# A fused RWKV, MoE and SoLU kernel: a unit's y moves one MLP step forward, next to its state update

## The chip, the cores and the metric

The kernel runs on one core of a Trainium2 chip. The metric is device time in microseconds (us) of one execution, the median of several runs.

## The reference, cut to what matters

```python
for t in range(S):                                  # S = 768, batch 4, 8 heads of 48
    cur = einsum('bhd,bhe->bhde', u[None] * kt, vt)
    y[:, :, t] = einsum('bhd,bhde->bhe', rt, state + cur)
    state = wt[:, :, :, None] * state + einsum('bhd,bhe->bhde', kt, vt)
x = y.transpose(0, 2, 1, 3).reshape(3072, 384)
h = x @ w_in                                        # 384 -> 2048
x = (h - tanh(h)) @ w_out                           # 2048 -> 384
h = x @ w_in2                                       # 384 -> 1024
solu = h * softmax(h)
out = layernorm(solu, eps=1e-6) * g_ln @ w_out2     # 1024 -> 384
```

## The kernel before, in words

The recurrence is cut into 24 units of 128 time steps (`C`), six to a batch row. A unit is five pieces of work. `att_0` brings w and r into the transposed form, makes the running product of w (`inc`) and scales r with it (`rh`). `att_1` makes the scaled k (`kh`). `att_2` puts the diagonal into `aq` on GpSimd, multiplies kh with rh on TensorE (`qk`), writes the masked products into `aq` on VectorE (line 303), transposes kh (`kt`), and copies that to `kn` on ScalarE. `att_3` multiplies kn with v (`ds`) and adds that to the old state, which gives the next state `st`; the last unit of a batch row has no such work. `att_4` makes y out of rh times the old state (line 340) and aq times v (line 343). It then copies y as a rounded high part and a rest into `xs` and `x3` (ScalarE lines 345 and 346, VectorE lines 347 and 348), and moves x3 into the 16-row remainders of xs with six DMAs (line 351). The old state that att_4 reads is the one from which att_3 starts; the two write and read different state buffers.

The first MLP works on blocks of 512 tokens, four units each, in 16 steps of 128 hidden columns: 96 steps in all, numbered s. In step s, `part1` multiplies xs of the block with the weights `wa` (`hp`, 9 matmuls of 512 columns). ScalarE, VectorE and GpSimd then make g out of hp (lines 386 to 398; VectorE's two instructions are lines 387 and 392). `part2` multiplies the g of step s-2 with the second weights (`x2p`, 9 matmuls), and adds up in three PSUM banks. There are two hp buffers and three g buffers. In the first and the last block the polynomial goes through hp itself, so hp is held until line 392 has read it; in the others line 387 is its last reader.

The attention of the first four units is done ahead of the MLP. That of units 4 to 23 is spread over the MLP's steps by the loop below, four steps to a unit, and always works for the block behind the one that is being multiplied. `xs` has two buffers, one for even blocks and one for odd ones. A block's first hp can start only when the DMAs of its last unit (units 7, 11, 15, 19, 23) have landed in xs. In the first 14 steps the loop also loads and converts the first MLP's weights (`conv_a`: DMA into `raw`, ScalarE line 121, VectorE lines 129 to 131, ScalarE line 134, GpSimd line 135 into `wa`). `raw` has two buffers. In the last block the second MLP's weights are converted in the same way (`conv_b`). The second MLP stage follows (lines 466 and 544), and is not touched.

The written order is not what the engines get: a scheduler reorders the instructions of each engine by a modelled time, with the written order as priority. All DMAs are issued by SyncE's queue (SP), which issues them in that scheduled order and holds each until what it waits for is done.

Of the kernel before, what the change touches and what calls it, by code (L numbers as in the profile page):

```python
# [559 lines left out]
@with_exitstack  # L560
def rwkv_moe_moe_kernel(ctx: ExitStack, tc: tile.TileContext, *args):
    nc = tc.nc
    K = Kern(tc, args)
    const = ctx.enter_context(tc.tile_pool(name="const", bufs=1))
    dram = ctx.enter_context(tc.tile_pool(name="dram", bufs=1, space=bass.MemoryType.DRAM))
    K.x2d = dram.tile([DM, NT], F32, name="x2d")
    safe = fast_path(tc, K, const)
    ok = nc.values_load(safe, min_val=0, max_val=1)
    with tc.If(ok < 1):
        general_path(tc, K, const)  # L570


def fast_path(tc, K, const):
    nc = tc.nc

    def pool(stack, name, bufs=1, side=None, **kw):
        return stack.enter_context(tc.tile_pool(name=name, bufs=bufs, side=side, reuse_waits="tile", **kw))

    K.load_act_set()
    K.setup(const)  # L580
    K.gl = const.tile([128, NM2], F32, name="gl")
    L, R, R2 = ExitStack(), ExitStack(), ExitStack()
    cv = pool(L, "cv", 2)
    cvr = pool(L, "cvr", 2)
    K.gp = pool(L, "gp", 2)
    K.gs = pool(L, "gs", 3)
    wp = pool(L, "wp")
    xp1 = pool(L, "xp1")
    xp0 = pool(R, "xp0", side="right")
    att = pool(R, "att", side="right")  # L590
    ps_x = pool(L, "ps_x", space=PSUM)
    K.ps_h = pool(L, "ps_h", 2, space=PSUM)
    K.ps_a = pool(R, "ps_a", 3, side="right", space=PSUM)
    K.wa = wp.tile([128, 2, NM, 2 * DM], F32R, name="wa")
    K.x2p = [ps_x.tile([128, BLK], F32, name=f"x2p{d}") for d in range(KM)]
    K.att_setup(att, xp0, xp1)
    K.setup_mask(K.kh[0])

    raw, gs = {}, {}
    OFF = -18  # L600
    LAST = (NB - 1) * NM
    nc.sync.dma_start(out=K.ub, in_=K.u.rearrange("h d -> (h d)").partition_broadcast(128))
    nc.scalar.activation(K.ub, K.ub, AF.Copy, scale=-1.0)
    K.att_load(0)
    K.att_load(1)
    nc.sync.dma_start(out=K.gl, in_=K.g_ln.rearrange("(k p) -> p k", p=128))

    early = 2
    when = (0, 2, 3, 5, 6, 8, 9, 11)
    SK = 2.1  # L610
    first = [(k + SK * u, K.att_pre if k < 0 else getattr(K, f"att_{k}"), u) for u in range(UB) for k in range(-1, 5)]
    first += [(SK * (u - 2) + 1.05, K.att_load, u) for u in range(2, UB + 2)] + [(SK * UB - 1, K.att_pre, UB)]
    first += [(2.0 * m, lambda m: K.conv_a(cv, cvr, m), m) for m in range(early)]
    for _, f, n in sorted(first, key=lambda e: e[0]):
        f(n)
    for s in range(-2, NB * NM + 2):
        if 0 <= s < NB * NM:
            gs[s] = K.part1(*divmod(s, NM))
        for k in (4, 0, 1, 2, 3):
            u, rem = divmod(s - OFF - k, 4)  # L620
            if rem == 0 and UB <= u < NU:
                getattr(K, f"att_{k}")(u)
        u, rem = divmod(s - OFF + 1, 4)
        if rem == 0 and UB < u < NU:
            K.att_pre(u)
        u, rem = divmod(s - OFF + 6, 4)
        if rem == 0 and UB + 1 < u < TURN:
            K.att_load(u)
        u, rem = divmod(s - OFF + 3, 4)
        if rem == 0 and TURN <= u < NU:  # L630
            K.load_turned(u)
        if 0 <= s - 2 < NB * NM:
            K.part2(*divmod(s - 2, NM), gs.pop(s - 2))
        if 0 <= s < NM - early:
            K.conv_a(cv, cvr, s + early)
        if s == LAST:
            R.close()
            wb = pool(R2, "wb", side="right")
            K.bx = pool(R2, "bx", 2, side="right")
            K.wb = wb.tile([128, 2, NM2, 2 * DM], F32R, name="wb")  # L640
            ps_r = pool(R2, "ps_r", side="right", space=PSUM)
        if s - LAST in when:
            with tc.issue_after(K.last_dve.ins), tc.issue_after(K.last_act.ins):
                K.conv_b(cv, cvr, when.index(s - LAST))
        if s == LAST + NM - 2:
            big = [
                cvr.tile([128, 2, DM, 2], U32, tag="raw", name=x).rearrange("p i f two -> p (i f two)")
                .bitcast(F32)[:, 0:FF2].rearrange("p (f x) -> p f x", f=2)
                for x in ("e0", "so0")
            ]  # L650
            K.ps_b, K.exps = (ps_r,), []
            small = K.ub.rearrange("p h d -> p (h d)")
            hs = {0: K.b_h(K.load_x2(0), 0, None, (small[:, 0:8], small[:, 8:40], *big))}
        n, due = divmod(3 * (s - NM), 7)
        if 0 <= n < NM + NM2 and due < 3:
            K.check_pair(cvr, n)
    safe = K.safe_flag(const)
    L.close()

    K.bs = pool(L, "bs", 5)  # L660
    K.bp = pool(L, "bp", 3)
    K.dso = pool(L, "dso", 3, space=bass.MemoryType.DRAM)
    ps_l = pool(L, "ps_l", space=PSUM)
    ps_t = pool(L, "ps_t", space=PSUM)
    K.ps_b = (ps_r, ps_t, ps_l)
    ts = {}
    for n in range(NTT + 3):
        if n < NTT:
            if n > 0:
                hs[n] = K.b_h(K.load_x2(n), n, (lambda: ts.update({n - 2: K.b_w(ts[n - 2])})) if n >= 2 else None)  # L670
            if K.shuffled(n):
                ts[n] = K.b_s(hs[n][0])
        if 0 <= n - 1 < NTT and not K.shuffled(n - 1):
            ts[n - 1] = K.b_t(hs[n - 1][0])
        if 0 <= n - 3 < NTT:
            K.b_o(n - 3, ts.pop(n - 3), hs.pop(n - 3)[1])
    L.close()
    R2.close()
    return safe
# [196 lines left out]
```

## Time and profile before

| | us |
|---|---|
| median of 3 runs | 796.96 (796.57 to 797.53) |
| the profiled execution, its own time | 795.77 |
| span of the profiled execution | 794.0 |
| TensorE busy with matmuls | 738.7 |
| VectorE, ScalarE, GpSimd busy | 592.7, 498.3, 418.7 |
| mean granted TensorE clock, share of full | 0.985 |

The span is what the trace shows; the profiled execution's own time is 1.77 us more. TensorE is the busiest engine by far, and is idle for the remaining 55.3 us of the span.

### The profile page before, as it was taken

What the parts mean: (1) busy time and instruction counts of PE and PEld (TensorE: products, weight loads), DVE (VectorE), ACT (ScalarE), POOL (GpSimd) and SP (SyncE); (2) the same over time, 40 slices, a digit from 0 to 9 for tenths busy, and PEclk for the clock granted to TensorE, in tenths of its full rate; (3) what the DMA queues carried; (4) which work ended last, traced back from release to release, by engine and by line L of the source; (5) the groups of instructions that cost most, each with busy time, mean ns of one, the idle gap of its engine ahead of it and who ended that gap; (6) DMA issues with size and microseconds to landing.
All of it is one profiled execution on the core that took longest, in us unless ns stands there. A gap on an engine that the chain in (4) does not pass through costs nothing. (4 is left out here: it accounts for less than half of the span.)

```text
span 794.0 us, 13215 instructions
## 1 busy us (share of the span) xinstructions
PE 738.7 (93%) x4338; PEld 604.9 (76%) x4338; DVE 592.7 (75%) x1023; ACT 498.3 (63%) x944; POOL 418.7 (53%) x389
## 2 busy tenths in 40 slices
PE   3677989889999999999999999999999999999997
PEld 2565767668887777778787777776878899898886
DVE  4689978777786677767676676368559999989982
ACT  3435776587776776687767765588736455554552
POOL 3544656556665555557555565366715544555440
PEclk9978998999999999999999999999999999999999
DMA  9965663867567575776646530043034554655531
GB/s 162 180 100 126 130 178 87 194 164 192 138 154 174 167 173 138 174 185 164 173 126 192 145 95 26 29 137 108 13 123 167 178 183 154 191 177 168 182 104 45
DMA packets 178158, 113.12 MB, mean 142 GB/s; under 512 B 95520, under 2 KB 166816, under 8 KB 178080
## 3 DMA queue, kind: packets, MB, share of 16 engines
q1 hardware_dynamic: 178080, 112.19, 54.1%
q8 instruction: 36, 0.59, 0.3%
q14 instruction: 42, 0.34, 0.2%
HBM read 88.81 MB, written 20.97 MB: 138 GB/s over the span
## 5 line engine op out<-in xcount | busy, mean ns | idle before, releaser
L381 PE MATMUL hp<-xs,wa 128*128 128x512 f32 x864 | 222.0, 400 | 9.6 <-DVE y L392 3.9
L405 PE MATMUL x2p<-g,wa 128*128 128x512 f32 x864 | 224.0, 399 | 6.7 <-ACT g L395 4.4
L381 PEld LDWEIGHTS hp<-xs,wa 128*128 128x128 f32 x864 | 162.5, 191 | 49.4 <-POOL wa L135 7.9
L405 PEld LDWEIGHTS x2p<-g,wa 128*128 128x128 f32 x864 | 158.2, 188 | 46.1 <-ACT g L395 6.0
L398 POOL TENSOR_TENSOR g<-y,g 128x512 fp32r<-128x512 f32 x96 | 128.5, 1339 | 39.3 <-ACT g L395 30.4
L387 DVE TENSOR_TENSOR y<-hp,t 128x512 f32<-128x512 f32 x96 | 65.6, 685 | 87.5 <-ACT t L386 86.2
L466 PE MATMUL h<-wb,x2s 128*128 128x512 f32 x432 | 106.1, 399 | 2.4 <-POOL x2s L451 2.4
L544 PE MATMUL o<-wb,ts 128*128 128x384 f32 x576 | 104.7, 335 | 1.0 <-POOL ts L523 1.0
L393 ACT ACTIVATE q<-t,cst 128x512 f32<-128x512 f32 x96 | 69.4, 723 | 53.7 <-DVE y L392 53.2
L544 PEld LDWEIGHTS o<-wb,ts 128*128 128x128 f32 x576 | 100.4, 188 | 3.3 <-POOL ts L523 1.3
L466 PEld LDWEIGHTS h<-wb,x2s 128*128 128x128 f32 x432 | 80.7, 188 | 21.8 <-POOL x2s L451 3.3
L397 POOL TENSOR_SCALAR g<-y 128x512 fp32r<-128x512 f32 x64 | 39.6, 619 | 94.7 <-DVE y L392 90.9
L386 ACT ACTIVATE t<-hp 128x512 f32<-128x512 f32 x96 | 56.5, 590 | 36.2 <-PE hp L381 35.7
L523 POOL TENSOR_TENSOR ts<-tw,ts 128x512 fp32r<-128x512 f32 x44 | 58.1, 1342 | 7.2 <-ACT ts L522 7.1
L392 DVE SCALAR_TENSOR_TENSOR y<-q,y 128x512 f32<-128x512 f32 x64 | 54.7, 855 | 6.7 <-ACT q L390 3.1
L451 POOL TENSOR_TENSOR x2s<-x2s 128x384 fp32r<-128x384 f32 x24 | 24.3, 1014 | 51.0 <-ACT x2s L450 51.0
L135 POOL TENSOR_TENSOR wa<-cv_x,wa 128x768 fp32r<-128x768 f32 x16 | 29.4, 1834 | 41.0 <-ACT wa L134 35.2
L495 ACT ACTIVATE e<-so 128x1024 f32<-128x1024 f32 x24 | 25.4, 1060 | 39.0 <-DVE so L494 39.0
L390 ACT ACTIVATE q<-t,cst 128x512 f32<-128x512 f32 x64 | 46.3, 724 | 1.6
L519 DVE STREAM_TRANSPOSE tw<-sw 128x1024 f32<-128x1024 f32 x22 | 44.6, 2028 | 0.5
L292 POOL TENSOR_SCALAR_AFFINE_SELECT aq<-dg 128x1024 f32<-128x1024 f32 x24 | 27.2, 1135 | 31.3 <-PE y L343 29.7
L286 POOL TENSOR_TENSOR inv<-inc,kh 112x512 f32<-112x512 f32 x24 | 30.5, 1273 | 23.5 <-ACT kh L278 17.9
(134 smaller groups left out, 1191.5 us busy)
## 6 DMA issues: line engine op xcount, KB each, us to landing
raw<-in_moe_w_out_dram SPq DMA_DIRECT2D x48, 384.0 KB, 4.1
dso<-so SPq DMA_DIRECT2D x22, 512.0 KB, 3.0
sw<-dso SPq DMA_DIRECT2D x88, 128.0 KB, 3.0
raw<-in_moe_w_in_dram SPq DMA_DIRECT2D x64, 144.0 KB, 3.4
rkw<-in_r_dram SPq DMA_DIRECT2D x64, 96.0 KB, 2.7
rkw<-in_k_dram SPq DMA_DIRECT2D x64, 96.0 KB, 2.6
rkw<-in_w_dram SPq DMA_DIRECT2D x64, 96.0 KB, 2.5
raw<-in_moe_w_in_dram SPq DMA_DIRECT2D x16, 384.0 KB, 3.8
```

The costliest lines, as they stand in the source:

```text
L381: self.mm(hp, self.wa[:, a, m, j * 128:(j + 1) * 128], xs[:, b, j], start=n == 0, stop=n == len(seq) - 1)
L386: nc.scalar.activation(t, hp, AF.Square)
L387: v.tensor_tensor(y, hp, t, ALU.mult)
L390: nc.scalar.activation(p, t, AF.Square, bias=self.c_fsb, scale=F_S)
L392: self.last_dve = v.scalar_tensor_tensor(y, p, F_E, y, ALU.add, ALU.mult)
L393: self.last_act = nc.scalar.activation(q, t, AF.Relu, bias=self.c_t2, accum_out=self.flags[:, col:col + 1])
L398: g.tensor_tensor(gs[:, 1], y, gs[:, 0], ALU.subtract)
L405: self.mm(self.x2p[d], self.wa[:, a, m, sl], gs[:, b], start=m == 0 and n == 0, stop=m == NM - 1 and n == 2)
L466: self.mm(p[:, f], xs[:, a, j], w, start=q == 0, stop=q == 8)
L519: self.turned = nc.vector.transpose(x.rearrange("p k (t b) -> p b k t", b=4), sw)
L523: nc.gpsimd.tensor_tensor(ts[:, 1, k], x[:, k], ts[:, 0, k], ALU.subtract)
L544: self.mm(p, ts[:, a, k], self.wb[:, b, k, DM:], start=q == 0, stop=q == 3 * NM2 - 1)
```

## The change

`att_4` of a unit is written into the step of `att_3` of the same unit, directly behind it, where before it stood in the step after that, ahead of `att_0` of the next unit. Nothing is added or removed: the same matmuls, copies and DMAs are issued, one step earlier in the written order, and the scheduler makes a new order out of that. The first four units are in another list, which does not change.

```diff
     for s in range(-2, NB * NM + 2):
         if 0 <= s < NB * NM:
             gs[s] = K.part1(*divmod(s, NM))
-        for k in (4, 0, 1, 2, 3):
-            u, rem = divmod(s - OFF - k, 4)
+        for d, k in ((0, 0), (1, 1), (2, 2), (3, 3), (3, 4)):
+            u, rem = divmod(s - OFF - d, 4)
             if rem == 0 and UB <= u < NU:
                 getattr(K, f"att_{k}")(u)
```

On TensorE, in the middle of the second block (unit 9, whose v is `vt_121`; `xs_139` is the odd blocks' xs), this is the order before:

```order
L381 MATMUL hp<-xs_139,wa 128x512 x9
L405 MATMUL x2p_116<-g,wa 128x512 x3
L405 MATMUL x2p_117<-g,wa 128x512
L317 MATMUL ds<-vt_121,kn 64x48
...
L405 MATMUL x2p_117<-g,wa 128x512 x2
L405 MATMUL x2p_118<-g,wa 128x512 x3
L381 MATMUL hp<-xs_139,wa 128x512 x9
L340 MATMUL y<-rh_127,st_134 64x128
...
L405 MATMUL x2p_116<-g,wa 128x512 x3
```

and this is the order of the change at the same place:

```order
L381 MATMUL hp<-xs_139,wa 128x512 x9
L405 MATMUL x2p_116<-g,wa 128x512 x3
L405 MATMUL x2p_117<-g,wa 128x512 x3
L405 MATMUL x2p_118<-g,wa 128x512
L317 MATMUL ds<-vt_121,kn 64x48
...
L340 MATMUL y<-rh_127,st_134 64x128
...
L405 MATMUL x2p_118<-g,wa 128x512 x2
L381 MATMUL hp<-xs_139,wa 128x512 x9
```

The 16 matmuls of y now follow the 8 of ds with nothing between them; before, 5 matmuls of x2p and 9 of hp stood between. All 13 units of the four middle blocks that have a ds read like this in the change; before, y stood 9 to 14 matmuls behind ds in nearly all of them.

On TensorE, at the end of the second block (y of unit 11, with `vt_123`, into `xs_138`, and the first hp that reads it), this is the order before:

```order
L343 MATMUL y<-aq,vt_123 48x128
L405 MATMUL x2p_116<-g,wa 128x512 x3
L405 MATMUL x2p_117<-g,wa 128x512 x3
L405 MATMUL x2p_118<-g,wa 128x512 x3
L381 MATMUL hp<-xs_139,wa 128x512 x9
L405 MATMUL x2p_116<-g,wa 128x512 x3
L405 MATMUL x2p_117<-g,wa 128x512 x3
L405 MATMUL x2p_118<-g,wa 128x512 x3
L301 MATMUL qk<-rh_126,kh_128 128x128 x5
L381 MATMUL hp<-xs_138,wa 128x512 x3
```

and this is the order of the change:

```order
L343 MATMUL y<-aq,vt_123 48x128
L405 MATMUL x2p_117<-g,wa 128x512 x2
L405 MATMUL x2p_118<-g,wa 128x512 x3
L381 MATMUL hp<-xs_139,wa 128x512 x9
...
L381 MATMUL hp<-xs_139,wa 128x512 x9
...
L301 MATMUL qk<-rh_126,kh_128 128x128 x2
...
L381 MATMUL hp<-xs_138,wa 128x512 x6
```

Between the end of y and the block's first hp there were 27 matmuls of 512 columns and 5 of qk; now there are 41 (5, 9, 9, 9 and 9) and 2 of qk.

On VectorE, in the first block, around the state update of unit 6 (line 325 waits for ds; line 131 ends a half of a weight conversion and frees `raw`), this is the order before:

```order
L392 SCALAR_TENSOR_TENSOR y<-hp,y 128x512
L131 ISA cv_x<-raw,cv_a 128x768
L130 SCALAR_TENSOR_TENSOR cv_a<-raw,cv_a 128x384
L129 TENSOR_SCALAR cv_a<-raw 128x384
L325 TENSOR_TENSOR st_134<-ds,inc_124 48x4x48 x2
L131 ISA cv_x<-raw,cv_a 128x768
```

and this is the order of the change:

```order
L392 SCALAR_TENSOR_TENSOR y<-hp,y 128x512
L130 SCALAR_TENSOR_TENSOR cv_a<-raw,cv_a 128x384
L245 TENSOR_REDUCE dg_136<-inv 128x4x2
L131 ISA cv_x<-raw,cv_a 128x768
L129 TENSOR_SCALAR cv_a<-raw 128x384
L130 SCALAR_TENSOR_TENSOR cv_a<-raw,cv_a 128x384
L131 ISA cv_x<-raw,cv_a 128x768
L325 TENSOR_TENSOR st_134<-ds,inc_124 48x4x48 x2
```

The instructions of the conversion that stood behind the state update now stand ahead of it.

## Rows read from the trace of the kernel before

**Rows 1.** The page: busy time, share of the span and instructions of each engine.

```profile
PE 738.7 (93%) x4338; PEld 604.9 (76%) x4338; DVE 592.7 (75%) x1023; ACT 498.3 (63%) x944; POOL 418.7 (53%) x389
```

**Rows 2.** Busy time of each engine in stretches, TensorE first: first, fourth and last block.

```profile
66.40:162.80 96.40, 84.22 (x489) 64.84 (x488) 79.25 (x162) 66.21 (x125) 56.03 (x41) 0.95 0.61 148
...
337.00:421.00 84.00, 83.90 (x539) 66.96 (x538) 59.58 (x104) 62.58 (x126) 50.51 (x51) 1.00 0.64 165
...
505.90:571.70 65.80, 61.89 (x264) 48.34 (x263) 44.41 (x53) 53.40 (x101) 39.22 (x23) 1.00 0.25 85
```

**Rows 3.** What TensorE waited for: us in total, times, longest.

```profile
PE hp L381 <- DVE y L392: 3.9, 4, 1.7
PE hp L381 <- POOL wa L135: 3.5, 3, 2.4
...
PE hp L381 <- DMA xs<-x: 2.0, 2, 1.3
```

**Rows 4.** Timeline, TensorE, end of the second block: start, us, instruction, idle before.

```profile
243.19 0.39 PE L343 MATMUL y<-aq,vt 128*48 128x128 f32 x4
...
252.11 0.93 PE L381 MATMUL hp<-xs,wa 128*128 128x512 f32 x3 [1.32 <-DMA xs<-x]
```

**Rows 5.** Timeline, SyncE's DMA queue, at the same place.

```profile
248.05 4.48 SPq L351 DMA_DIRECT2D xs<-x  x6
```

**Rows 6.** Timeline, TensorE, end of the fourth block.

```profile
412.39 0.39 PE L343 MATMUL y<-aq,vt 128*48 128x128 f32 x4
...
421.63 0.93 PE L381 MATMUL hp<-xs,wa 128*128 128x512 f32 x3 [0.73 <-DMA xs<-x]
```

**Rows 7.** Timeline, TensorE, start of the last block.

```profile
502.08 4.05 PE L405 MATMUL x2p<-g,wa 128*128 128x512 f32 x17
505.98 0.84 PE L381 MATMUL hp<-xs,wa 128*128 128x512 f32 x3
...
513.71 2.34 PE L381 MATMUL hp<-xs,wa 128*128 128x512 f32 x9 [1.23 <-DVE y L392]
```

**Rows 8.** Timeline, ScalarE and VectorE, at the same place.

```profile
509.57 0.60 ACT L386 ACTIVATE t<-hp 128x512 f32<-128x512 f32 x1 [4.25 <-PE hp L381]
...
512.98 0.68 DVE L392 SCALAR_TENSOR_TENSOR y<-hp,y 128x512 f32<-128x512 f32 x1
```

**Rows 9.** Timeline, TensorE, a middle block around qk of unit 10.

```profile
206.98 2.20 PE L405 MATMUL x2p<-g,wa 128*128 128x512 f32 x9
209.02 2.20 PE L381 MATMUL hp<-xs,wa 128*128 128x512 f32 x9
...
211.83 1.16 PE L301 MATMUL qk<-rh,kh 48*128 48x128 f32 x16
```

**Rows 10.** Timeline, VectorE, the second masked copy of that unit.

```profile
215.98 0.73 DVE L303 COPY_PREDICATED aq<-mask,qk 128x512 f32<-128x512 uint8 x1
```

**Rows 11.** Timeline, TensorE, first block.

```profile
118.97 1.65 PE L405 MATMUL x2p<-g,wa 128*128 128x512 f32 x3 [2.18 <-ACT g L395]
120.41 4.04 PE L381 MATMUL hp<-xs,wa 128*128 128x512 f32 x9
...
162.80 2.37 PE L381 MATMUL hp<-xs,wa 128*128 128x512 f32 x9 [2.36 <-POOL wa L135]
```

**Rows 12.** Timeline, VectorE, first block, state update of unit 6.

```profile
125.12 0.72 DVE L325 TENSOR_TENSOR st<-ds,inc 48x192 f32<-48x192 f32 x2 [2.46 <-PE ds L318]
125.87 0.55 DVE L131 CUSTOM_DVE_ANT_0 cv_x<-raw,cv_a 128x768 uint16<-128x768 uint16 x1
```

**Rows 13.** Timeline, SyncE's DMA queue, first block.

```profile
126.49 0.31 SPq L361 DMA_DIRECT2D raw<-in_moe_w_in_dram  x1
...
133.10 4.57 SPq L351 DMA_DIRECT2D xs<-x  x6
...
141.39 0.58 SPq L361 DMA_DIRECT2D raw<-in_moe_w_in_dram  x1
```

**Rows 14.** Busy time by stretch, first block: TensorE's granted clock is the seventh figure.

```profile
120.00:124.00 4.00, 4.00 (x11) 2.96 (x9) 2.65 (x6) 2.00 (x4) 4.00 (x4) 0.50 0.00 0
```

## Prediction

> **What bounds the kernel now.** I read the page first: TensorE is busy for 738.7 of 794.0 us [rows 1], and no other engine comes near that. A change that adds no work can then only act through TensorE's idle time, so the next view is busy time by stretch. Idle is length less busy. The first block has 96.40 - 84.22 = 12.18 us of it, the fourth only 0.10, the last 65.80 - 61.89 = 3.91 [rows 2]. The reader is to see two regimes: in the middle blocks TensorE runs without a gap, and the other engines' order is free as long as nothing comes late; in the first block TensorE often waits for others. The third view is TensorE's waits. Among those of hp are 2.0 us in two waits for the DMAs of xs, 3.9 us in four for line 392, and 3.5 us in three for converted weights [rows 3]. The timeline then gives each wait its place.
>
> **The change part by part.** The work is the same, so its busy time costs nothing. What is priced is where waits go.
>
> *End of the second block.* The last y of unit 11 starts at 243.19 and ends at 243.58; the block's first hp starts at 252.11 after a wait of 1.32 us for the DMAs [rows 4]. So 8.53 us pass from the end of y until the data is there: copies on ScalarE and VectorE, six DMAs of which the first is issued at 248.05 [rows 5], and their landing. Nine 512-column matmuls take 209.02 - 206.98 = 2.04 us when they follow one another, 0.227 us each [rows 9]. The new order puts 41 of them behind y, 41 x 0.227 = 9.3 us, and two matmuls of qk besides. As 9.3 is more than 8.53, the wait goes: -1.32 us, with 0.8 us to spare. Its bounds are 0 (the copies come that much later in the new order) and -1.32.
>
> *End of the fourth block.* y of unit 19 ends at 412.39 + 0.39 = 412.78, and hp starts at 421.63 after 0.73 us of waiting [rows 6]: 8.85 us. The new order again has 41 matmuls, 9.3 us. The wait goes with 0.45 us to spare: -0.73 us, bounds 0 and -0.73.
>
> *Start of the last block.* Here the old order put 17 matmuls of x2p in front of the block's first three of hp [rows 7], and then hp of two steps almost without x2p between. The third hp then had only one row of nine matmuls in front of it, and waited 1.23 us for line 392 of the first [rows 7], since hp is held until that instruction in this block. From the first hp's square on ScalarE at 509.57 to the end of line 392 at 512.98 + 0.68 = 513.66 is 4.09 us [rows 8]. In the new order y of unit 23 is 41 matmuls ahead of the block, x2p and hp alternate by nines, and 27 matmuls or 27 x 0.227 = 6.1 us lie between the first hp and the third. 6.1 is more than 4.09: -1.23 us, bounds 0 and -1.23.
>
> Together these three are 1.32 + 0.73 + 1.23 = 3.28 us.
>
> *The middle of the blocks.* y now stands directly behind ds, 5 x2p and 9 hp or 14 x 0.227 = 3.2 us earlier. TensorE takes its queue in order, so if aq is not written by then, hp and x2p behind y wait too. For unit 10, qk starts at 211.83 [rows 9] and the second masked copy ends at 215.98 + 0.73 = 216.71 [rows 10], 4.9 us later. In the new order qk (1.1 us to the last matmul's end), kt (0.4, as its four are half as many as qk's), 9 x2p, 9 hp, 4 x2p (22 x 0.227 = 5.0) and ds (about 0.6) stand ahead of y: 7.1 us. The slack shrinks from 5.4 to 2.2 us and stays positive: 0.
>
> *The DMAs of the moved step.* Six per unit move ahead on SyncE's queue, which holds what is behind them. In the middle blocks the loads behind them are for a unit later and nothing on TensorE waits for them: 0. In the first block it matters which conversion loads stand behind. Before, a load's first DMAs were issued, then the six (4.57 us from 133.10), and the rest of that load from 141.39 [rows 13]. In the new order the six stand ahead of all of that load, but its last DMA has the same set ahead of it as before, and unit 6's y is six matmuls (1.4 us) earlier on TensorE. The Trainium skill, "DMA: Bandwidth & Descriptors", section "Anatomy of one DMA", speaks against the change here: a semaphore wait is served on the issuing sequencer, before dispatch, so a waiting DMA holds what is behind it. The gap up to 141.39 in [rows 13] agrees with that. By it alone the sum would be the same, as the last DMA decides.
>
> *The first block.* This is the term I can't read off. Its end hangs on the converted weights: hp of its last step waits 2.36 us for them at 162.80 [rows 11]. That chain was held up at unit 6's state update: VectorE stood 2.46 us waiting for ds at 125.12, the conversion's line 131 came only at 125.87 [rows 12], and the next raw load could be issued only at 126.49 [rows 13]. In the new order line 131 stands ahead of line 325, so that load can go about 2.46 + 0.75 = 3.2 us earlier. How much of this arrives at the end is bounded by what TensorE waited for weights, 3.5 us in three waits [rows 3]; the other end is a new stall. Such a stall is in the trace: 2.18 us at 118.97, after which nine hp took 4.04 instead of 2.20 us [rows 9, 11], and so 4.0 us in all with 1.84 of slow clock. I take -1.0, under a third of 3.5, because the order of ScalarE and of SyncE's queue changes here too and the next stage of the chain may be late instead. Both ends, -3.5 and +4.0, are kept for the range.
>
> *The clock.* After 2.18 us of idle the next stretch ran at a granted clock of 0.50, which is the 1.2 GHz level [rows 14]. After the 1.32 us wait the three hp took 0.93 us together [rows 4], like full speed. So the block-end waits that go are worth their own length only. [...]
>
> **The sum.** -3.28 - 1.0 = -4.3 us. Against the profiled execution that is 795.77 - 4.3 = 791.5 us; its span would be 789.7. The median of the runs shown is 1.19 us above that execution, so the prediction is 796.96 - 4.3 = 792.7 us. A measurement of this kernel can tell about 0.2% or 1.6 us from no change.
>
> **The rivals.**
>
> *The waits are moved, not removed.* The time that TensorE gains at a block's end is lost at the next place where g or the weights are late: the last block has 3.91 us of idle, 2.7 of them elsewhere than at its start. For it: there VectorE and ScalarE carry the weight conversion and may set the pace. Against it: in the middle blocks nothing is late at all. Then only 1.32 + 0.73 or less stays, the first block gives nothing, and the time is 795 to 797: 796 us.
>
> *A new stall in the first block.* One stall like that at 118.97, in front of a stretch of slow clock, costs 4.0 us and eats the gain: 796.96 - 3.28 + 4.0 = 797.7. For it: TensorE has x2p of one step more ahead of hp in several places of the new order there, and so less to do when g is late. Against it: the conversions are ahead of the state update.
>
> *y waits for aq (slower).* With the slack at 2.2 us, masked copies that come 2.5 us later than before would make TensorE wait 0.3 us for each of the 16 units in the middle blocks: 4.8 us, which outweighs 3.28. It decides from there: at 3 us later, it is 16 x 0.8 = 12.8 us, and 796.96 - 3.3 + 12.8 = 806.5. For it: VectorE gets the state update, the running product and y's copies in one stretch now. Against it: the masked copies stand ahead of that stretch, not behind it.
>
> *The change does nothing*, since the scheduler would reorder anyway: excluded by the orders shown.
>
> **How the numbers follow.** The forecast, with the three waits gone and a first block between -3.5 and +1, holds 0.65, and spans 790 to 795. Waits moved: 0.17. A new stall: 0.11. y waits for aq: 0.07. Faster by over 0.2% (below 795.4): all of the forecast, a third of the moved waits, a little of the new stall: 0.72. Slower (above 798.6): y's wait and a third of the new stalls: 0.11. The rest, 0.17, is within 0.2%. For the range I reach down to 789.5 (the forecast with the whole of 3.5 us) and up to 798, which takes in the moved waits and the milder half of the new stalls, and leaves out about 2 in 10.
>
> **What would show it.** In the changed trace, no wait of hp for the DMAs of xs at the ends of the second and fourth block, no wait of the third hp in the last block, and the middle blocks with no idle time in front of y. In the first block, line 131 ahead of the state update of unit 6, the load behind it issued near 123, and a shorter wait for weights at the last hp. The prediction is wrong if waits of y for aq show up in every unit, or if the first block is longer than 97 us.

## The result, and the profile after

| | before | after |
|---|---|---|
| median, us | 796.18 (791.63 to 797.53, 6 runs) | 787.09 (784.36 to 788.07, 6 runs) |
| span of the profiled execution | 794.0 | 786.3 |

The ratio is 0.9883, with an interval of 0.9854 to 0.9911: 1.2% or some 9.3 us faster. The forecast was -4.3 us and 792.7, with a range from 789.5. The direction was right, the size less than half.

The page's busy times of the changed kernel answer to [rows 1]:

```profile
PE 738.8 (94%) x4338; PEld 607.7 (77%) x4338; DVE 576.1 (73%) x1023; ACT 495.4 (63%) x944; POOL 418.4 (53%) x389
```

TensorE's busy time is the same, so the 7.7 us between the two spans are idle time and what goes with it. To find where, I cut both traces at the same products: the first hp, the first x2p of step 20, that of step 79 and that of step 95. Between two cuts from step 20 on, TensorE does exactly the same products in both kernels (the trace has 1062 records of the MLP's and 860 of the attention's from step 20 to 79), which the cuts at hp of [rows 2] don't give, since the new order also changes how far hp runs ahead of x2p. Busy time by stretch: length first, then TensorE's busy time, and as the seventh figure the granted clock, the share of TensorE's full clock that it was given. Before:

```profile
66.39:202.77 136.38, 124.20 (x761) 96.94 (x760) 109.86 (x216) 97.35 (x187) 79.44 (x63) 0.96 0.62 153
202.77:510.28 307.51, 305.46 (x1924) 243.03 (x1923) 210.55 (x365) 212.03 (x428) 174.39 (x172) 1.00 0.57 143
510.28:582.37 72.09, 68.18 (x291) 53.09 (x289) 49.41 (x60) 58.28 (x108) 42.58 (x25) 1.00 0.24 80
```

and after:

```profile
65.18:201.88 136.70, 126.00 (x761) 98.51 (x760) 108.84 (x217) 97.15 (x188) 79.77 (x64) 0.95 0.66 153
201.88:506.68 304.80, 304.80 (x1924) 243.37 (x1922) 205.27 (x365) 211.28 (x431) 174.67 (x171) 1.00 0.57 144
506.68:574.69 68.01, 66.69 (x292) 53.74 (x290) 45.63 (x58) 55.70 (x104) 42.93 (x25) 1.00 0.26 85
```

The lengths give the account of this pair: 66.39 to 65.18, -1.21 ahead of the first hp; 136.38 to 136.70, +0.3 in the first block and four steps behind it; 307.51 to 304.80, -2.71 in the middle; 72.09 to 68.01, -4.08 in the last block; nothing behind it. In the middle the 2.05 us of idle (307.51 - 305.46) are gone, as forecast, and another 0.66 with them. The last block gave over three times the forecast's 1.23: its idle time went from 3.91 to 1.32 us, and its busy time, for the same products at the same clock, from 68.18 to 66.69.

The waits of TensorE after, for [rows 3], hold none of hp for the DMAs of xs and none for the weights:

```profile
PE hp L381 <- DVE y L392: 4.8, 4, 2.5
...
PE x2p L405 <- POOL g L398: 2.7, 4, 1.0
```

The ends of the second and the fourth block, for [rows 4] and [rows 6], in TensorE's timeline: the first hp of each block (249.95 and 415.88) follows without a wait.

```profile
248.46 1.66 PE L405 MATMUL x2p<-g,wa 128*128 128x512 f32 x6
249.95 1.55 PE L381 MATMUL hp<-xs,wa 128*128 128x512 f32 x6
...
413.84 2.20 PE L405 MATMUL x2p<-g,wa 128*128 128x512 f32 x9
415.88 0.86 PE L381 MATMUL hp<-xs,wa 128*128 128x512 f32 x3
```

The last block, for [rows 7], also TensorE's timeline: hp and x2p alternate by nines from the start, and two waits of over 0.1 us are left in the whole block.

```profile
500.56 2.20 PE L381 MATMUL hp<-xs,wa 128*128 128x512 f32 x9
502.60 2.20 PE L405 MATMUL x2p<-g,wa 128*128 128x512 f32 x9
...
533.04 1.66 PE L405 MATMUL x2p<-g,wa 128*128 128x512 f32 x6 [0.67 <-POOL g L398]
...
546.19 1.67 PE L405 MATMUL x2p<-g,wa 128*128 128x512 f32 x6 [0.61 <-POOL g L398]
```

Before, the wait of 1.23 us [rows 7] was followed by four more of over 0.2 us in that block (and two of about 0.1):

```profile
525.94 1.65 PE L405 MATMUL x2p<-g,wa 128*128 128x512 f32 x6 [0.61 <-POOL g L398]
...
539.27 1.67 PE L405 MATMUL x2p<-g,wa 128*128 128x512 f32 x6 [0.60 <-POOL g L398]
...
549.83 2.35 PE L381 MATMUL hp<-xs,wa 128*128 128x512 f32 x9 [0.26 <-DVE y L392]
...
553.88 1.66 PE L405 MATMUL x2p<-g,wa 128*128 128x512 f32 x6 [1.01 <-POOL g L398]
```

In the first block the new order does what the prediction read from it. VectorE runs line 131 ahead of the state update, which waits 0.59 instead of 2.46 us [rows 12]:

```profile
121.11 0.54 DVE L131 CUSTOM_DVE_ANT_0 cv_x<-raw,cv_a 128x768 uint16<-128x768 uint16 x1
...
122.98 0.56 DVE L131 CUSTOM_DVE_ANT_0 cv_x<-raw,cv_a 128x768 uint16<-128x768 uint16 x1
124.13 0.72 DVE L325 TENSOR_TENSOR st<-ds,inc 48x192 f32<-48x192 f32 x2 [0.59 <-PE ds L318]
```

SyncE's queue issues the raw load behind it at 121.72, where before it was 126.49, and the six DMAs of xs from 127.36 instead of 133.10 (for [rows 13]):

```profile
121.72 0.31 SPq L361 DMA_DIRECT2D raw<-in_moe_w_in_dram  x1
...
127.36 3.78 SPq L351 DMA_DIRECT2D xs<-x  x6
```

But TensorE has other waits there in place of those of [rows 11], the first of them with slow products behind it (nine hp in 3.67 us):

```profile
110.95 3.67 PE L381 MATMUL hp<-xs,wa 128*128 128x512 f32 x9 [2.50 <-DVE y L392]
...
149.04 1.65 PE L405 MATMUL x2p<-g,wa 128*128 128x512 f32 x3 [1.65 <-ACT g L395]
```

### The profile page after: what moved, and what is told of

It reads as the page before. It is cut to its first block, busy times and chain, and to the rows that moved or that the text cites. A ratio compares the mean times of both kernels' runs of the same rounds, so it can differ in the third digit from the quotient of the medians.

```text
span 786.3 us, 13215 instructions
## 1 busy us (share of the span) xinstructions
PE 738.8 (94%) x4338; PEld 607.7 (77%) x4338; DVE 576.1 (73%) x1023; ACT 495.4 (63%) x944; POOL 418.4 (53%) x389
## 5 line engine op out<-in xcount | busy, mean ns | idle before, releaser
L381 PEld LDWEIGHTS hp<-xs,wa 128*128 128x128 f32 x864 | 164.4, 192 | 44.0 <-POOL wa L135 5.2
L523 POOL TENSOR_TENSOR ts<-tw,ts 128x512 fp32r<-128x512 f32 x44 | 56.3, 1301 | 7.4 <-ACT ts L522 7.1
L392 DVE SCALAR_TENSOR_TENSOR y<-q,y 128x512 f32<-128x512 f32 x64 | 49.9, 779 | 4.4 <-ACT q L390 1.2
L286 POOL TENSOR_TENSOR inv<-inc,kh 112x512 f32<-112x512 f32 x24 | 29.6, 1233 | 32.9 <-ACT kh L278 24.2
L497 POOL TENSOR_TENSOR st<-st,cst 128x1 f32<-128x1 f32 x23 | 12.6, 549 | 55.8 <-DVE st L496 44.6
```

The lines of the kernel that those rows point to most:

```text
L381: self.mm(hp, self.wa[:, a, m, j * 128:(j + 1) * 128], xs[:, b, j], start=n == 0, stop=n == len(seq) - 1)
L392: self.last_dve = v.scalar_tensor_tensor(y, p, F_E, y, ALU.add, ALU.mult)
L523: nc.gpsimd.tensor_tensor(ts[:, 1, k], x[:, k], ts[:, 0, k], ALU.subtract)
```

## Experiments

Below, "first", "middle" and "last" are the three stretches above, of each kernel's profiled execution. The kernels differ in the written order alone, so the same few lines of the loop are edited each time; the diffs are against the kernel before, unless they show a line of the experiment ahead of them.

The first four ask which units make the gain. Theory A: a block's inputs are there before its first hp, so only the last unit of each block counts. Theory B: the first block's chain of weight conversions. Theory C: y behind ds gains a little at every unit.

**Only the last units of the blocks (7, 11, 15, 19, 23).**

```diff
+        for d, k in ((4, 4), (0, 0), (1, 1), (2, 2), (3, 3), (3, 4)):
+            u, rem = divmod(s - OFF - d, 4)
+            if rem == 0 and UB <= u < NU and (k < 4 or (d < 4) == (u % UB == UB - 1)):
```

> y is moved for the last unit of each block only (units 7, 11, 15, 19, 23); the other 15 units stay as before. Theory A, the gain is that a block's inputs land before its first hp: nearly the whole gain is here, 1.2% less some 0.3%, so 5.5 to 9 us faster than before, with no wait of hp for the DMAs of xs and none of the third hp of the last block. Theory B, the gain is in the first block, where the conversion of the weights gets ahead of the state update: unit 6 is not moved and the first block's order is the old one, so at most 3.3 us faster. Theory C, y directly behind ds is by itself better everywhere: 5 of 20 units, about 2.3 us.

Ratio 0.9933 (0.9901 to 0.9964), about -5.3 us. Its middle and last stretch:

```profile
199.57:506.15 306.58, 306.58 (x1924) 243.21 (x1923) 213.68 (x367) 214.57 (x432) 174.60 (x172) 1.00 0.56 143
506.15:574.15 68.00, 66.63 (x291) 53.77 (x289) 45.62 (x58) 55.77 (x104) 42.83 (x25) 1.00 0.25 85
```

No idle is left in the middle, and the last block is that of the change. But the middle is only 0.93 us shorter than before, although 2.05 us of idle are gone: its busy time rose from 305.46 to 306.58 at the same products and the same full clock.

**All moved units but those.**

```diff
-            if rem == 0 and UB <= u < NU and (k < 4 or (d < 4) == (u % UB == UB - 1)):
+            if rem == 0 and UB <= u < NU and (k < 4 or (d < 4) == (u % UB < UB - 1)):
```

> The opposite: y is moved for the 15 units that are not the last of their block. Theory A: within 0.4% of before, and the waits of 1.32, 0.73 and 1.23 us are back at the starts of the third, fifth and last block. Theory B: unit 6 is moved, so the first block keeps its gain, 4 to 7 us faster. Theory C: three quarters of 9.3 us, 7 us.

Ratio 0.9936 (0.9905 to 0.9966), about -5.1 us, where A alone gives nothing. The last block is as long as before, 72.12. In its profile the first stretch is 133.18 us (before 136.38) and the middle 305.34 (before 307.51), the latter with one wait for the DMAs of 1.12 us left.

**The units of the second block alone (4 to 7), which are worked on during the first.**

```diff
+            if rem == 0 and UB <= u < NU and (k < 4 or (d < 4) == (u < 2 * UB)):
```

> y is moved for units 4 to 7 only, which are worked in the first block. Theory A: no change, 0 within 2 us; the last block has its 3.9 us of idle time as before. Theory B: 5 to 7 us faster, all of it before the second block starts. What the first block gives by itself is the term of the prediction that was put at -1.0 us.

Ratio 0.9981 (0.9948 to 1.0013): not told from no change. Its first stretch is 133.77 us, shorter than before, but the middle is 310.53, longer. The reason stands in the clock: behind the wait for the DMAs at the end of the second block, 1.08 us here, the granted clock was 0.50 for 6.8 us.

```profile
250.30:257.10 6.80, 6.80 (x19) 4.86 (x20) 2.84 (x4) 1.78 (x4) 0.01 (x1) 0.50 0.98 202
```

**The units from 8 on.**

```diff
+            if rem == 0 and UB <= u < NU and (k < 4 or (d < 4) == (u >= 2 * UB)):
```

> y is moved for units 8 to 23, the first block keeps its old order. Theory A: 6 to 9 us faster, nearly the whole gain. Theory B: 3.3 us, only the three waits at block ends. Together with the run before, the two should add up to the gain of the whole change, 9.3 us, if they are independent.

Ratio 0.9897 (0.9851 to 0.9943), about -8.2 us. Middle 304.80 and last 68.01, the lengths of the change; first 139.63, none of its gain. The two halves add up: the last units and the rest to -10.4 us, units 4 to 7 and the rest to -9.7. B is out as the main cause. A and C are each half right by these four, so I counted what else differs between the orders.

What differs is the number of **separate stretches** of the attention's short products between the MLP's 512-column ones: rows of short products in TensorE's queue, not the three stretches of time above. Behind step 16 the order of before has 52 of them, the change 44. One unit of the third block, before:

```profile
282.44 1.79 PE L381 MATMUL hp<-xs,wa 128*128 128x512 f32 x7
284.16 0.26 PE L317 MATMUL ds<-vt,kn 128*64 128x48 f32 x1
...
284.75 0.74 PE L381 MATMUL hp<-xs,wa 128*128 128x512 f32 x2
285.42 0.43 PE L340 MATMUL y<-rh,st 112*64 112x128 f32 x4
...
287.33 2.34 PE L405 MATMUL x2p<-g,wa 128*128 128x512 f32 x9
289.50 2.26 PE L381 MATMUL hp<-xs,wa 128*128 128x512 f32 x9
```

and the same unit after:

```profile
280.34 0.40 PE L381 MATMUL hp<-xs,wa 128*128 128x512 f32 x1
280.67 0.26 PE L317 MATMUL ds<-vt,kn 128*64 128x48 f32 x1
...
283.04 2.12 PE L381 MATMUL hp<-xs,wa 128*128 128x512 f32 x8
285.00 2.23 PE L405 MATMUL x2p<-g,wa 128*128 128x512 f32 x9
287.06 2.26 PE L381 MATMUL hp<-xs,wa 128*128 128x512 f32 x9
```

Both show nine hp, ds, y and nine x2p: 289.50 - 282.44 = 7.06 us before, 287.06 - 280.34 = 6.72 after. TensorE is never idle in either. The two hp that stood alone between ds and y took 285.42 - 284.75 = 0.67 us, where two of a row of nine take 2 x 0.227 = 0.45 [rows 9]: the first product behind a stretch and the last one ahead of the next are each 0.1 us longer, and leaving a stretch takes 0.15 to 0.20.

So two theories went into the next runs. W: only TensorE's waits count. S: the waits, and 0.33 us for each separate stretch.

**Unit 23 alone, the entry of the last block.**

```diff
+            if rem == 0 and UB <= u < NU and (k < 4 or (d < 4) == (u == NU - 1)):
```

> y moved for unit 23 alone, the last unit of the fifth block, so that only the entry of the last block changes. Since the first four runs two theories are left. W: the gain is TensorE's waits alone (the two at block ends, and in the last block all five waits, which sum to 4.5 us over a plain spacing before and 1.6 after, since hp and x2p then alternate evenly there). S: the waits, and besides them the number of separate stretches of the attention's short products between the MLP's 512-column ones; each costs about 0.33 us (last MLP product before it 0.32, exit 0.15 to 0.20, first product behind it 0.335, against 0.23 plain). W: -2.9 us. S: -2.2 us (two stretches more, 54 against 52, since y of this unit is cut up). What the prediction said of this entry: -1.2. The two block-end waits of 1.3 and 0.7 us stay.

Ratio 0.9959 (0.9931 to 0.9987), about -3.3 us. The interval reaches from -1.0 to -5.5 us and holds all three forecasts, so the profile has to decide. One unit's y makes the whole gain of the last block, 72.09 to 68.22, and nothing in the middle (307.91):

```profile
508.70:576.92 68.22, 66.65 (x291) 53.72 (x289) 45.63 (x58) 55.74 (x104) 43.44 (x25) 1.00 0.26 85
```

**y in the earlier step, but behind part2, away from ds.**

```diff
-        for k in (4, 0, 1, 2, 3):
+        for k in (0, 1, 2, 3):
...
             K.part2(*divmod(s - 2, NM), gs.pop(s - 2))
+        u, rem = divmod(s - OFF - 3, 4)
+        if rem == 0 and UB <= u < NU:
+            K.att_4(u)
```

> Every y is moved into the earlier step as in the change, but written behind part2 of that step, so that x2p products stand between ds and y: TensorE has 54 stretches of attention products behind step 16, as before 52, the change 44. The block-end and last-block order is as even as in the change. W: the same gain as the change, about -9 us with what the first block gives. S: the change's gain less ten stretches at 0.33 us: about -6, and from step 17 to the last hp some 3.3 us more than the change (395.0 us there, 401.0 before).

Ratio 0.9943 (0.9919 to 0.9967), about -4.5 us. The middle is without idle, as in the change, and yet 2.1 us longer; from step 17 to the last hp it takes 398.4 us, where S said 3.3 above 395.0. W fell here: the middle of the change took 304.80 us in each of its two profiles and in that of the run with the units from 8 on, so 2.1 us are well clear of its scatter.

```profile
200.53:507.44 306.91, 306.91 (x1924) 242.82 (x1923) 207.35 (x363) 214.06 (x430) 173.31 (x171) 1.00 0.56 142
```

**ds moved back to y.**

```diff
-        for k in (4, 0, 1, 2, 3):
-            u, rem = divmod(s - OFF - k, 4)
+        for d, k in ((4, 3), (4, 4), (0, 0), (1, 1), (2, 2)):
+            u, rem = divmod(s - OFF - d, 4)
```

> The reverse: y stays in its later step, and ds is moved into that step, directly ahead of y. TensorE has 37 stretches behind step 16 (before 52, the change 44); the order at block ends and at the entry of the last block is that of before, so the waits there stay. W: 0 us. S: 15 stretches at 0.33 us: about -5 us, with the waits of 1.3 and 0.7 us at block ends and all five of the last block still there; from step 17 to the last hp about 396 us against 401.0 before.

Ratio 1.0012 (0.9983 to 1.0042). S missed by 5 to 6 us, and the profile has a reason: the wait for the DMAs grew to 2.20 us, and the clock behind it was 0.50 for 10.2 us, which is worth about 5 (half of them). The other executions point the same way: the mean granted clock of the twelve is 0.977, where that of the kernel before in the same set is 0.982.

```profile
254.95 1.62 PE L381 MATMUL hp<-xs,wa 128*128 128x512 f32 x3 [2.20 <-DMA xs<-x]
```

```profile
254.90:265.10 10.20, 10.15 (x28) 7.07 (x29) 2.84 (x4) 2.77 (x7) 2.33 (x4) 0.50 0.65 139
```

The middle is 307.69 with that loss in it. That its stretches saved 5 us is then only worked out; this run alone decides nothing between W and S.

**All other work of a unit one step earlier.** This one shifts `OFF` and keeps ds and y at the step that the change gives them; within a step they are now written ahead of the next unit's work.

```diff
-    OFF = -18
+    OFF = -19
...
-    for s in range(-2, NB * NM + 2):
+    for s in range(-3, NB * NM + 2):
...
+        for d, k in ((4, 3), (4, 4), (0, 0), (1, 1), (2, 2)):
+            u, rem = divmod(s - OFF - d, 4)
```

> ds and y together as in the change and at the same steps, but everything that a unit does ahead of them (inputs, scan, qk, kt) one step earlier: 32 stretches behind step 16 (two for each of the 16 units), and more products between the last y of a block and the first hp of the next than in the change (45 to 58 against 33 to 43). W: as the change, about -9 us. S: twelve stretches fewer than the change: 4 us below it, about -13 us against before, unless the earlier start costs more in the first block, where it presses on the PSUM banks and on VectorE: up to +4 there.

Ratio 0.9942 (0.9917 to 0.9968), about -4.6 us. The middle is 300.24, 4.6 us below the change, about what S said, and that with one wait of 1.06 us for g in it; the first stretch is 144.19, some 7 to 10 us longer than in the change where +4 was allowed for, and so the whole missed.

**The same for the units from 7 on only.**

```diff
+        for d, k in ((3, 3), (3, 4), (0, 0), (1, 1), (2, 2)):
+            for early in (0, 1):
+                u, rem = divmod(s - OFF - d + early * (k < 3), 4)
+                if rem == 0 and UB <= u < NU and (early > 0) == (u >= 7):
+                    getattr(K, f"att_{k}")(u)
```

> The change, with the inputs, scan, qk and kt one step earlier for the units from 7 on only, so that the first block is nearly that of the change: 34 stretches behind step 16 against 44 of the change. S (0.33 us for each stretch): from step 17 to the last hp 390.3 us against 393.6 of the change at the same number of products and 401.0 before; the whole 3.3 us below the change, so about -12 us against before, if the first block stays at 101 us. W (waits only): as the change, -9 us. What could spoil it is the first block, where the last eighth run lost 8 us; up to +4 here.

Ratio 0.9892 (0.9860 to 0.9923), about -8.6 us. Middle and last are the shortest of all, and the first stretch loses as before (145.47 us):

```profile
208.50:507.58 299.08, 299.08 (x1924) 242.18 (x1923) 212.46 (x365) 211.40 (x436) 176.27 (x173) 1.00 0.58 146
507.58:575.57 67.99, 66.64 (x291) 53.73 (x289) 45.61 (x58) 55.66 (x104) 42.99 (x25) 1.00 0.25 85
```

**The change and the kernel before, once more,** with no edit.

> The changed kernel once more, beside the others on one chip: about -9 us against before by its first measurement; by the account so far -5.2 us of waits, -2.2 us of stretches from step 17 on, and -1 to -2 in the first block, -8.4 to -9.4 in all.

Ratio 0.9836 (0.9806 to 0.9867), about -13 us against the seventeen executions of the kernel before beside it (median 799.14), and -11.1 against the twelve of the next run on the same chip (796.57). The lengths are 134.45, 304.80 and 68.09: the middle and the last block come out again to 0.1 us, the first does not.

```profile
503.22:571.31 68.09, 66.66 (x292) 53.74 (x290) 45.62 (x58) 55.70 (x104) 43.08 (x25) 1.00 0.25 85
```

> The kernel before as if it were a change: 0 us, with a second profile of it, for what differs between two executions of one program. All theories: the waits at the ends of the second and the fourth block and the five of the last block are there again, and 401 us from step 17 to the last hp; if the clock falls behind one of the block-end waits, as in two of the experiments, some 3 to 5 us more.

Ratio 0.9975 (0.9950 to 1.0001): a quarter of a per cent between two sets of runs of one program. The lengths are 139.20, 306.82 and 73.28. Both block-end waits were there again (1.10 and 0.24 us), and the clock stayed up behind them.

```profile
205.68:512.50 306.82, 305.48 (x1925) 242.97 (x1923) 211.38 (x365) 211.98 (x428) 174.21 (x172) 1.00 0.57 143
512.50:585.78 73.28, 68.32 (x291) 52.99 (x290) 50.66 (x60) 58.21 (x108) 42.42 (x25) 1.00 0.24 79
```

**A version meant to beat both:** the earlier step for the units from 9 on, which lie behind the first block; the load of unit 9 keeps its step.

```diff
-                if rem == 0 and UB <= u < NU and (early > 0) == (u >= 7):
+                if rem == 0 and UB <= u < NU and (early > 0) == (u >= 9):
```

> A version meant to beat both: the change, with the inputs, scan, qk and kt one step earlier for the units from 9 on, whose work lies behind the first block (the load of unit 9 keeps its step). TensorE then has 32 stretches of attention products behind step 16 (the change 44, before 52). S: between the first x2p of step 20 and that of step 79 about 299 us, as in the ninth run (the change 304.8, before 307.5), the last block 68.0 us as in the change (before 72.1), and the first block as in the change, since its units keep their steps: 5 to 6 us below the change, about -14 to -15 us against before. W: as the change, -9 to -11. Against it: unit 9's load has one step less, and if that is short, VectorE and TensorE wait for it once, 1 to 5 us.

Ratio 0.9849 (0.9819 to 0.9878), about -12 us, median 786.07 of 6 runs. That lies between the two ratios of the change (0.9883 and 0.9836), so it is not told from it.

```profile
64.65:204.43 139.78, 129.18 (x761) 99.10 (x761) 114.03 (x224) 97.52 (x186) 80.16 (x64) 0.95 0.69 158
204.43:503.51 299.08, 299.08 (x1923) 242.16 (x1922) 212.68 (x364) 210.93 (x436) 175.53 (x173) 1.00 0.58 146
503.51:572.34 68.83, 66.96 (x291) 53.57 (x289) 46.18 (x58) 55.74 (x104) 43.13 (x25) 1.00 0.25 84
```

The middle gives the 5.7 us below the change, and the first stretch, which is 3 to 5 us longer though the units of the first block were written as in the change, takes most of it back. The scheduler orders that part anew too: TensorE's order parts from that of the change at the tenth product of the stretch, and 20 more records of its products stand ahead of the hp of the first block's last step.

## Why the prediction was right and wrong

*The ends of the second and the fourth block* were right about the waits: both are gone, and the idle time of the middle went from 2.05 us (1.34 in the second profile of before) to 0. Their worth was not right. With the last units alone moved the idle time is 0 too, at the same 46 separate stretches, and the middle took 306.58 us, 0.93 and 0.24 below the two profiles of before.

*The middle of the blocks, priced at 0,* was wrong in its reason. y never waited for aq behind ds, so the rival in which it does is out; no such wait is in the middle of the changed trace, which has no idle at all there. But the place in the queue is not free where TensorE is never idle. In the unit shown, ds and y together save 0.34 us. The new order gives about half of such savings back, since it cuts other y and qk into more pieces: 46 stretches became 40 between steps 20 and 79, though 11 units with a ds lie there. From the last units alone to the whole change, the middle went from 306.58 to 304.80. Waits and order together gave 2.71 us in the first pair of profiles and 2.02 in the second, where 2.05 was forecast for the waits alone: that the sum came out is luck. The distance that the moved y jumps was taken at its largest, 14 matmuls: in the trace of before y stood 9 to 14 matmuls of the MLP behind ds in 8 of the 13 units, not in nearly all, and 1 to 8 in the other five.

*The start of the last block* is the step that failed. It was sized at the one wait that stands there, 1.23 us. It measured 72.09 - 68.01 = 4.08 us in the first pair of profiles and 73.28 - 68.09 = 5.19 in the second, and unit 23 alone brings it. Two things were left out. A wait costs more than the idle that is printed: nine x2p start at 510.28 and hp at 513.71, 3.43 us where 2.04 is plain [rows 7, 9], so the delay is 1.39 for 1.23 of idle, and the nine hp behind it take 2.18 to the next start. And the bunch of 18 hp at the entry left its mark on the rest of the block: the four later waits, 2.48 us together, became two of 1.28. The prediction had put the block's other 2.7 us of idle down as "elsewhere" and counted no gain from them. The two things together make up the term: added up over every place in this block where two products start more than 0.03 us further apart than a plain 0.229, the delays are 6.0 us before and 2.2 after, which is 3.8 of the 4.08. That the uneven entry makes part of the later waits is shown by unit 23 alone. Not all of them come from it: the two that are left stand in the x2p of steps 85 and 88, where the old order waits too (0.60 and 1.01 us); those that went stood in the x2p of step 82 and the hp of step 90. How the entry is handed on from step to step through ScalarE, VectorE and GpSimd is not shown.

*The first block, taken at -1.0 with bounds of -3.5 and +4.0,* was probably too small, and is still the least certain term. Over the five profiles with y of units 4 to 6 moved and the rest as in either kernel, the stretch up to step 20 took 136.70, 134.45, 133.18, 133.77 and 133.62, mean 134.3; over the four with all of units 4 to 7 as before, 136.38, 139.20, 139.63 and 135.41, mean 137.7. That is -3.3 us, with ranges that overlap; the first pair alone has +0.3. The run with the last units, where only unit 7 of these is moved, took 136.26 and is in neither group. The chain that the prediction named is there, no hp waits for weights any more, and the stall of the rival came as well: 2.50 us at 110.95 with slow products behind it. By its own sign the first block would have failed, since it took 164.02 - 65.18 = 98.8 us in the first profile against the limit of 97 (96.6 in the second). But that limit could not tell: the kernel before took 96.4 and 97.7.

Terms as forecast: -2.05 and 0 for the middle, -1.23, -1.0, in all -4.3. As measured: -2.0 to -2.7 for the middle with both its terms, -4.1 to -5.2, -3.3: some -9 to -11, against -9.3 by the first timing and -13 or -11 by the second. The lower end of the range, 789.5, is also a slip: the forecast with the whole of 3.5 us is 796.96 - 3.28 - 3.5 = 790.2. The time ahead of the first hp, from 63.0 to 66.9 us over all 14 profiles and in no relation to the edits, blurs each comparison.

*The clock.* As far as the clock goes, "worth their own length only" holds for the two profiles of before. It is no rule: of the five profiles in which hp is seen to wait for the DMAs at the end of the second block (1.32, 1.10, 1.12, 1.08 and 2.20 us), two have a granted clock of 0.50 behind it, the 1.2 GHz level, for 6.8 and 10.2 us. Of the nine other profiles, among them both of the change, none shows a fall in the middle (one of them has 0.68 us of idle at that place, put down to ScalarE). That the wait causes the fall is likely but not shown; why the same wait has one in some executions and not in others stays open.

*SyncE's queue.* The prediction read the gap up to 141.39 [rows 13] as a queue held by a waiting DMA. The trace of before has seven loads of w and r for the attention issued between the six DMAs and that load, from 138.08 to 141.35, so the gap is issuing and not waiting. The queue's waits are elsewhere: 29.6 us in nine waits of raw loads for line 131 between 60 and 170 us. The term stays at 0 by this.

## What to carry to other kernels

Where TensorE is the bound, size a removed wait by the whole stage behind it: here an uneven order at the entry of a stage with two buffers made part of the waits later in it, and the test is to compare two traces between the same products. A queue that is never idle can still lose time by its order: count how often short products break up a row of long ones. And a wait that the clock survived in one profile may be followed by a slow stretch in the next: here one of an estimated 3.4 and 5.1 us, half of the 6.8 and 10.2, behind waits of 1.08 and 2.20.

## What the runs showed of the hardware

A separate stretch of products of 48 to 128 columns between 512-column ones cost about 0.33 us in a TensorE without idle time: 0.32 instead of 0.23 for the last long product, 0.15 to 0.20 for leaving the stretch, 0.335 instead of 0.23 for the first long one behind it. With the same products and no idle, the middle took 306.91 us with 48 stretches (y away from ds), 306.58 with 46 (last units only), 304.80 with 40 (the change) and 299.08 with 28 (the two runs with the work of units from 7 or 9 on a step earlier): 0.39 us for each over the whole range, though only 0.26 from 48 to 40 and 0.48 from 40 to 28, so the number of stretches is not the whole of it.
